# Causal decay attention and a leaky-ReLU MLP in one kernel: another order for the list of operations, with other engines for some of them

## The chip, the cores and the metric

The kernel runs on one core of a Trainium2 chip. The time is the device time of one execution in microseconds, taken as the median of the runs shown. The core has five engines that run at once, each through its own instructions in order: TensorE (PE, with weight loads PEld), VectorE (DVE), ScalarE (ACT), GpSimd (POOL) and SyncE (SP), which here only issues DMAs. ACT and POOL issue DMAs too.

## What is computed

Attention with a decay per head (4 batches, 8 heads, 768 positions, head width 64) gives 3072 rows of 512 numbers; a two-layer MLP (512 to 2048 to 512) with a leaky ReLU is applied to them.

```python
for b in range(nb):                       # blocks of 64 positions
    intra = einsum('bhic,bhjc->bhij', qb, kb) * Dmask[None]
    intra = einsum('bhij,bhjd->bhid', intra, vb)
    inter = einsum('bhid,bhde->bhie', qb * lam_pow[None], kv_state)
    out[:, :, sl] = intra + inter
    kv_state = lam_block * kv_state + einsum('bhsd,bhse->bhde', kb * rev_pow[None], vb)
x = out.transpose(0, 2, 1, 3).reshape(3072, 512)
h = x @ w_in
g = maximum(h, 0.0) + alpha * minimum(h, 0.0)
return g @ w_out
```

Dmask holds lam to the power of the distance where it is not negative, and zero elsewhere; the other factors are powers of lam as well.

## The kernel before

**Tiling.** The tokens are worked in six chunks c of 512: 256 positions of two batches. The attention of a chunk is four units: two batches times two halves of the heads. There are 24 units, numbered through, so units 8 to 11 are chunk 2. A unit has two blocks of 128 positions, 0 and 1.

**One unit** goes through these steps. `load` (fp32) and `load16` (fp16) bring k, q and v in; a `hold` is a one-element write that keeps a load from starting before a place in DVE's list. `cast` makes one fp16 tile `qk16` of q and k. `turn_by_dma` transposes it with a DMA issued by SP into `qkT` (units 0 to 7 use `turn` on PE and a copy, `turned`). `decayed` scales the transposed q into `qdT`, `key_decayed` scales k into `kdec`. `cluster(old, new)` is a run of small matmuls in a PSUM tile `acc`: for the old unit the state part (from `RD` and `qdT`) and the product of masked scores with v, for the new unit the scores `s` and the state's increment. `masked` multiplies the scores by the decay mask, `state` makes the next state `R`, `spread` copies it into `RD`, and `out_of` copies a unit's result from PSUM into `xT`, the MLP's input.

**The MLP of a chunk**: for each of 16 tiles f of the hidden layer, `up` (four matmuls into one PSUM bank), `below` (ACT: the negative part), `gate` (DVE: the leaky ReLU in fp16). A bank is free for the next `up` once its `gate` is done. For chunks 0 to 2 `down` makes the second layer, a quarter of the sum a call, and `store` copies and sends the result. For chunks 3 to 5 the second layer is seven `product`s a pair of blocks instead of eight, for which sums of blocks of g and of w_out are needed: `weight_sum`, `weight_less`, `gate_sum`, or `gate_copied` and `gate_added` (the same sum made by DMAs, the second issued by POOL). `taken` copies or adds a product's PSUM into the result and issues the stores.

**What sets the order.** Nothing is scheduled by the program. The list of operations at the end of the function (from L659) is the order: each engine gets its own instructions in the order in which the list names them, and waits, inside an instruction, for what its data need. Last arguments choose the engine: "V" is DVE, "A" is ACT, "G" is POOL; a load with `ring=1` goes by POOL, without it by SP. The list's opening, to L795, is the same before and after but for one `hold`.

```python
def copy_on(eng, out, in_):              # casts, spreads, out_of, turned
    if eng == "A": nc.scalar.activation(out, in_, AF.Copy)
    elif eng == "V": nc.vector.tensor_copy(out=out, in_=in_)
    else: nc.gpsimd.tensor_copy(out=out, in_=in_)
```

`warm_up` writes a one on DVE and takes its logarithm on ACT (L179), for which ACT loads a function table; its result is read by nothing.

Of the kernel before, what the change touches and what calls it, by code (L numbers as in the profile page):

```python
# [11 lines left out]
def kernel(  # L12
# [434 lines left out]
    G = {}  # L447
# [322 lines left out]
    masked(3, 0)  # L770
    spread(3, 1, "A", True)
# [60 lines left out]
    below(0, 1, 1)
    below(0, 7, None)
    masked(4, 0)
    load_wout(0)
    decayed(4, "G")
    gate(0, 1, 1)
    gate(0, 7, None)
    up(0, 9, None, 0)
    below(0, 9, None)  # L840
    cluster(4, 5)
    masked(5, 1)
    gate(0, 9, None)
    up(0, 11, None, 2)
    below(0, 11, None)
    gate(0, 11, None)
    state(5, 0)
    cast(6, "k", "G")
    zeros(3, 0)
    state(5, 1)  # L850
    up(0, 14, None, 1)
    load("q", 2, 0, ring=1)
    spread(5, 1, "A")
    below(0, 14, None)
    gate(0, 14, None)
    decayed(5, "G")
    up(0, 12, None, 0)
    up(0, 10, None, 2)
    masked(5, 0)
    below(0, 10, None)  # L860
    turn(6)
    up(0, 15, None, 1)
    out_of(4, "A")
    cluster(5, None)
    key_decayed(6, "G")
    gate(0, 10, None)
    cast(7, "k", "V")
    up(0, 13, None, 2)
    below(0, 12, None)
    turned(6, "V")  # L870
    below(0, 15, None)
    out_of(5, "A")
    turn(7)
    gate(0, 12, None)
    load_wout(2)
    up(1, 0, 0, 0)
    below(0, 13, None)
    cluster(None, 6)
    below(1, 0, 0)
    gate(0, 15, None)  # L880
    down(0, 2, 0, 1)
    gate(1, 0, 0)
    up(1, 2, 0, 0)
    gate(0, 13, None)
    below(1, 2, 0)
    hold("k", 2, 1)
    turned(7, "A")
    down(0, 2, 1, 2)
    masked(6, 1)
    up(1, 1, 0, 2)  # L890
    state(6, 0)
    load_wout(3)
    gate(1, 2, 0)
    decayed(6, "G")
    key_decayed(7, "V")
    below(1, 1, 0)
    gate(1, 1, 0)
    cast(9, "q", "V")
    decayed(7, "V")
    down(0, 1, 0, 0)  # L900
    spread(6, 1, "A")
    cast(9, "k", "V")
    down(0, 1, 1, 2)
    masked(6, 0)
    down(0, 0, 0, 2)
    down(0, 0, 1, 1)
    down(0, 0, 2, 1)
    state(6, 1)
    down(0, 1, 2, 2)
    cluster(6, 7)  # L910
    out_of(6, "A")
    down(0, 0, 3, 1)
    cast(8, "k", "V")
    load("k", 2, 1, ring=1)
    spread(9, 0, "V")
    load16("v", 2, 0)
    state(7, 0)
    cast(8, "q", "V")
    down(0, 2, 2, 2)
    down(0, 2, 3, 2)  # L920
    turn_by_dma(8)
    store(0, 0)
    spread(7, 1, "A")
    key_decayed(8, "G")
    store(0, 2)
    up(1, 3, 0, 2)
    below(1, 3, 0)
    masked(7, 0)
    masked(7, 1)
    state(7, 1)  # L930
    cast(10, "k", "V")
    weight_sum(1, 0)
    cluster(7, 8)
    masked(8, 1)
    key_decayed(9, "G")
    gate(1, 3, 0)
    down(0, 1, 3, 2)
    out_of(7, "A")
    up(1, 4, None, 1)
    turn_by_dma(9)  # L940
    store(0, 1)
    state(8, 0)
    below(1, 4, None)
    decayed(8, "G")
    load("q", 2, 1)
    key_decayed(10, "G")
    masked(8, 0)
    spread(8, 1, "G")
    up(1, 5, None, 0)
    state(8, 1)  # L950
    cluster(8, 9)
    below(1, 5, None)
    load("q", 3, 0)
    cast(11, "k", "V")
    up(1, 0, 1, 2)
    gate(1, 4, None)
    below(1, 0, 1)
    gate(1, 5, None)
    up(1, 1, 1, 1)
    below(1, 1, 1)  # L960
    gate(1, 0, 1)
    cast(10, "q", "A")
    up(1, 6, None, 0)
    cast(11, "q", "V")
    down(0, 3, 0, 2)
    gate(1, 1, 1)
    up(1, 7, None, 1)
    below(1, 6, None)
    load16("v", 3, 0)
    weight_sum(1, 1)  # L970
    down(0, 3, 1, 2)
    below(1, 7, None)
    gate(1, 6, None)
    masked(9, 1)
    load16("v", 2, 1)
    key_decayed(11, "V")
    up(1, 8, None, 0)
    state(9, 0)
    below(1, 8, None)
    down(0, 3, 2, 2)  # L980
    down(0, 3, 3, 2)
    turn_by_dma(10)
    cast(12, "q", "V")
    load("k", 3, 0)
    masked(9, 0)
    gate(1, 8, None)
    up(1, 11, None, 0)
    spread(9, 1, "A")
    decayed(9, "G")
    gate(1, 7, None)  # L990
    turn_by_dma(11)
    out_of(8, "V")
    store(0, 3)
    up(1, 10, None, 1)
    spread(13, 0, "A")
    decayed(10, "V")
    key_decayed(12, "G")
    below(1, 11, None)
    state(9, 1)
    below(1, 10, None)  # L1000
    cast(12, "k", "V")
    up(1, 13, None, 2)
    gate(1, 11, None)
    cluster(9, 10)
    below(1, 13, None)
    up(1, 9, None, 0)
    gate(1, 10, None)
    load("k", 4, 0)
    below(1, 9, None)
    up(1, 15, None, 1)  # L1010
    gate(1, 13, None)
    state(10, 0)
    load("k", 3, 1)
    load("q", 4, 0)
    gate(1, 9, None)
    below(1, 15, None)
    up(1, 12, None, 2)
    turn_by_dma(12)
    below(1, 12, None)
    up(1, 14, None, 0)  # L1020
    gate(1, 15, None)
    masked(10, 0)
    out_of(9, "A")
    cast(13, "q", "G")
    down(1, 0, 0, 1)
    below(1, 14, None)
    gate(1, 12, None)
    cast(13, "k", "G")
    down(1, 0, 1)
    decayed(11, "G")  # L1030
    up(1, 2, 1, 2)
    gate(1, 14, None)
    up(1, 3, 1, 0)
    down(1, 0, 2)
    spread(11, 0, "G")
    down(1, 0, 3)
    below(1, 3, 1)
    cast(14, "k", "G")
    key_decayed(13, "G")
    spread(10, 1, "V")  # L1040
    state(10, 1)
    spread(10, 0, "A")
    masked(10, 1)
    cluster(10, 11)
    spread(14, 0, "V")
    load("q", 3, 1)
    key_decayed(15, "G")
    gate(1, 3, 1)
    below(1, 2, 1)
    gate(1, 2, 1)  # L1050
    state(11, 0)
    cast(16, "k", "A")
    masked(11, 0)
    spread(11, 1, "V")
    state(11, 1)
    load("q", 5, 0)
    turn_by_dma(13)
    masked(11, 1)
    out_of(10, "A")
    store(1, 0)  # L1060
    down(1, 2, 0, 2)
    load("q", 4, 1, ring=1)
    cast(16, "q", "G")
    decayed(13, "G")
    cast(15, "k", "V")
    down(1, 2, 1)
    down(1, 2, 2)
    turn_by_dma(16)
    down(1, 2, 3)
    store(1, 2)  # L1070
    cluster(11, 12)
    warm_up()
    down(1, 1, 0, 1)
    down(1, 1, 1)
    spread(12, 0, "G")
    state(12, 0)
    spread(12, 1, "V")
    out_of(11, "A")
    up(2, 2, None, 2)
    decayed(12, "G")  # L1080
    up(2, 0, None, 0)
    down(1, 1, 2)
    down(1, 1, 3)
    state(12, 1)
    below(2, 0, None)
    cast(14, "q", "A")
    below(2, 2, None)
    key_decayed(16, "V")
    load16("v", 3, 1)
    masked(12, 1)  # L1090
    weight_sum(2, 0)
    cast(17, "q", "G")
    store(1, 1)
    gate(2, 0, None)
    up(2, 3, None, 0)
    gate(2, 2, None)
    up(2, 1, None, 1)
    below(2, 1, None)
    masked(12, 0)
    gate(2, 1, None)  # L1100
    key_decayed(14, "G")
    cluster(12, 13)
    weight_sum(2, 1)
    below(2, 3, None)
    gate(2, 3, None)
    cast(15, "q", "G")
    down(1, 3, 0, 2)
    load("k", 4, 1)
    state(13, 0)
    up(2, 4, None, 1)  # L1110
    turn_by_dma(14)
    cast(18, "q", "G")
    cast(19, "k", "A")
    below(2, 4, None)
    down(1, 3, 1)
    turn_by_dma(15)
    key_decayed(17, "V")
    down(1, 3, 2)
    masked(13, 1)
    gate(2, 4, None)  # L1120
    up(2, 5, None, 0)
    up(2, 6, None, 1)
    out_of(12, "A")
    spread(13, 1, "G")
    cast(19, "q", "V")
    below(2, 5, None)
    state(13, 1)
    below(2, 6, None)
    masked(13, 0)
    gate(2, 5, None)  # L1130
    cluster(13, 14)
    spread(15, 0, "G")
    up(2, 7, None, 0)
    gate(2, 6, None)
    below(2, 7, None)
    state(14, 0)
    load("k", 5, 1)
    state(14, 1)
    down(1, 3, 3)
    up(2, 8, None, 1)  # L1140
    out_of(13, "A")
    masked(14, 1)
    store(1, 3)
    masked(14, 0)
    below(2, 8, None)
    decayed(14, "G")
    spread(18, 0)
    gate(2, 7, None)
    spread(14, 1, "G")
    gate(2, 8, None)  # L1150
    cluster(14, 15)
    up(2, 9, None, 2)
    load("k", 5, 0)
    masked(15, 0)
    state(15, 0)
    up(2, 10, None, 0)
    below(2, 9, None)
    load16("v", 4, 0)
    up(2, 11, None, 1)
    below(2, 10, None)  # L1160
    gate(2, 9, None)
    turn_by_dma(19)
    gate(2, 10, None)
    up(2, 12, None, 2)
    decayed(15, "G")
    out_of(14, "A")
    key_decayed(19)
    state(15, 1)
    spread(15, 1, "A")
    up(2, 13, None, 0)  # L1170
    below(2, 12, None)
    masked(15, 1)
    below(2, 11, None)
    below(2, 13, None)
    gate(2, 12, None)
    load16("v", 5, 1)
    cluster(15, 16)
    gate(2, 11, None)
    out_of(15, "A")
# [396 lines left out]
```

## Time and profile before

| | |
|---|---|
| median of 3 runs | 214.49 us (213.87 to 215.24) |
| profiled execution, its own time | 213.43 us |
| its span, first to last instruction | 211.6 us |
| TensorE clock granted | 1.0 throughout |
| POOL busy after 160 us | 0.00 us |
| busy share of the 16 DMA engines, about 5 to 116 us | 0.8 to 0.9 and more in every slice |
| HBM read, written | 27.28 MB, 6.29 MB |

Busy shares of a span are averages over stages; "idle before" and the waits say what an engine stood for. A matmul's listed time includes the pipeline that the next one overlaps: four matmuls of 512 columns list 1.0 us together and follow the four before them by 0.86 to 0.88 us.

### The profile page before, as it was taken

What the parts mean: (1) busy time and instruction counts of PE and PEld (TensorE: products, weight loads), DVE (VectorE), ACT (ScalarE), POOL (GpSimd) and SP (SyncE); (2) the same over time, 40 slices, a digit from 0 to 9 for tenths busy, and PEclk for the clock granted to TensorE, in tenths of its full rate; (3) what the DMA queues carried; (4) which work ended last, traced back from release to release, by engine and by line L of the source; (5) the groups of instructions that cost most, each with busy time, mean ns of one, the idle gap of its engine ahead of it and who ended that gap; (6) DMA issues with size and microseconds to landing.
All of it is one profiled execution on the core that took longest, in us unless ns stands there. A gap on an engine that the chain in (4) does not pass through costs nothing.

```text
span 211.6 us, 5657 instructions
## 1 busy us (share of the span) xinstructions
PE 200.9 (95%) x2286; PEld 124.6 (59%) x2286; DVE 168.9 (80%) x347; ACT 112.7 (53%) x231; POOL 83.5 (39%) x122
## 2 busy tenths in 40 slices
PE   4798999999999999999999999999999999999992
PEld 4776555555555455455544545556666766766881
DVE  3799799999689994889988969999669778549731
ACT  3998576643647536455755556363464525354320
POOL 8989199170721570987960083213021000000000
PEclk9999999999999999999999999999999999999999
DMA  4999999998999999899999391867273211011213
GB/s 113 275 184 194 198 237 227 246 245 118 276 238 220 314 222 231 247 152 243 135 208 105 121 222 56 156 149 157 41 187 65 99 53 50 2 50 53 74 53 124
DMA packets 62443, 33.54 MB, mean 158 GB/s; under 512 B 34497, under 2 KB 58577, under 8 KB 62417
## 3 DMA queue, kind: packets, MB, share of 16 engines
q0 software_dynamic: 22096, 12.45, 41.1%
q1 hardware_dynamic: 38416, 17.57, 35.8%
q10 hardware_dynamic: 1904, 3.16, 4.4%
q8 instruction: 18, 0.29, 0.6%
q14 instruction: 9, 0.07, 0.1%
HBM read 27.28 MB, written 6.29 MB: 159 GB/s over the span
## 4 chain that ended last, share of the span: by engine, by line
PE 78%; ACT 9%; DVE 6%; DMA 4%; issue 2%; ACTq 0%; DVEq 0%; SPq 0%
PE h_ps L457 36%; PE p_ps L598 17%; PE o_ps L491 15%; PE s L362 3%; DVE g L481 3%; PE acc L374 2%; DMA qkT<-qk 2%; DMA lam_sb<-in_lam_dram 2%; ACT qkT L248 2%; PE acc L344 2%; ACT dmask L202 1%; DVE RD L250 1%; ACT qk L248 1%; PE acc L391 1%; DVE sm L403 1%
## 5 line engine op out<-in xcount | busy, mean ns | idle before, releaser
L457 PE MATMUL h_ps<-xT,w_in_sb 128*128 128x512 f16 (+1 forms) x416 | 92.8, 363 | 1.0 <-DVE g L481 0.6
L468 ACT ACTIVATE m<-h_ps 128x512 f32<-128x512 f32 (+1 forms) x104 | 57.5, 564 | 59.9 <-PE h_ps L457 55.0
L481 DVE SCALAR_TENSOR_TENSOR g<-m,oma,h_ps 128x512 f16<-128x512 f32 (+1 forms) x104 | 71.1, 702 | 19.3 <-ACT m L468 18.2
L457 PEld LDWEIGHTS <-w_in_sb 128*128 128x128 f16 x416 | 39.3, 98 | 38.9 <-issue 1.8
L491 PE MATMUL o_ps<-w_out_sb,g 128*128 128x512 f16 x192 | 45.9, 379 | 0.2 <-DVE g L481 0.2
L403 DVE TENSOR_TENSOR sm<-s,dmask 128x512 f16<-128x512 f32 x48 | 32.1, 684 | 2.2 <-PE s L362 2.1
L491 PEld LDWEIGHTS <-g 128*128 128x128 f16 x192 | 18.2, 98 | 20.7 <-issue 0.2
L321 POOL TENSOR_TENSOR qdT<-qkT,qdecay 128x512 f16<-128x512 f16 (+1 forms) x16 | 17.5, 1096 | 16.8 <-DMA qkT<-qk 13.0
L598 PEld LDWEIGHTS <-g 128*128 128x128 f16 x192 | 18.8, 98 | 4.8
L279 POOL TENSOR_TENSOR kdec<-kraw,kdecay 128x512 f16<-128x512 f32 x13 | 13.7, 1063 | 8.4 <-DMA kraw<-in_k_dram 8.3
L428 DVE SCALAR_TENSOR_TENSOR R<-R,rdecay,acc 128x64 f16<-128x64 f16 x60 | 13.8, 272 | 3.7 <-PE acc L391 1.9
L598 PEld LDWEIGHTS <-gsum 128*128 128x128 f16 x144 | 14.0, 98 | 3.1
L252 POOL COPY RD<-R 64x128 f16<-64x128 f16 x24 | 7.8, 324 | 16.2 <-DVE R L428 15.5
L622 ACT ACTIVATE o_sb<-p_ps 128x512 f32<-128x512 f32 (+1 forms) x16 | 7.6, 489 | 10.8 <-PE p_ps L598 10.8
L248 ACT ACTIVATE xT<-acc 128x512 f16<-128x512 f32 x15 | 8.9, 596 | 8.0 <-PE acc L391 5.4
L238 PE MATMUL op_fill<-ident 128*128 128x128 f16 x109 | 9.3, 253 | 3.0 <-POOL ident masks.py:199 2.7
L598 PE MATMUL p_ps<-wsum,gsum 128*128 128x256 f16 x96 | 12.0, 273 | 0.0
L598 PE MATMUL p_ps<-wsum,g 128*128 128x256 f16 x96 | 11.9, 272 | 0.0
L248 ACT ACTIVATE RD<-R 64x128 f16<-64x128 f16 x28 | 8.6, 306 | 6.1 <-DVE R L428 4.9
L598 PE MATMUL p_ps<-w_out_sb,g 128*128 128x256 f16 x96 | 11.6, 273 | 0.0
L102 POOL DMA_DIRECT2D vh<-in_v_dram x13 | 11.5, 890 | 0.0
L238 PEld LDWEIGHTS <-ident 128*128 128x128 f16 x109 | 8.4, 116 | 3.5 <-POOL ident masks.py:199 2.7
(87 smaller groups left out, 215.4 us busy)
## 6 DMA issues: line engine op xcount, KB each, us to landing
kraw<-in_k_dram SPq DMA_DIRECT2D x8, 512.0 KB, 5.7
out_dram<-o_sb ACTq DMA_DIRECT2D x12, 256.0 KB, 3.1
qraw<-in_q_dram SPq DMA_DIRECT2D x6, 512.0 KB, 7.3
out_dram<-o_sb SPq DMA_DIRECT2D x24, 128.0 KB, 2.0
vh<-in_v_dram POOLq DMA_DIRECT2D x11, 256.0 KB, 6.2
w_in_sb<-in_moe_w_in_dram POOLq DMA_DIRECT2D x4, 512.0 KB, 9.4
w_out_sb<-in_moe_w_out_dram POOLq DMA_DIRECT2D x4, 512.0 KB, 9.5
gsum<-g SPq DMA_DIRECT2D x6, 256.0 KB, 2.6
```

Of the source, the lines that this page charges most:

```text
L102: nc.gpsimd.dma_start(out=rows16(x, c, bi)[:, ds(h0, n), :], in_=source({"q": q, "v": v}[x], c, bi, h0, n))
L238: nc.tensor.matmul(t[:, 0:128], lhsT=ident, rhs=ident, start=True, stop=True)
L248: nc.scalar.activation(out, in_, AF.Copy)
L279: engine(eng).tensor_tensor(out=kdec, in0=kr, in1=d.unsqueeze(3).to_broadcast([128, 2, 4, D]), op=ALU.mult)
L321: engine(eng).tensor_tensor(out=x, in0=y, in1=d.unsqueeze(2).to_broadcast([128, 4, n, 64]), op=ALU.mult)
L403: nc.vector.tensor_tensor(out=t["sm"][hl], in0=t["s"][hl], in1=mask_of(hl, units[n][2]), op=ALU.mult)
L428: nc.vector.scalar_tensor_tensor(out=then[:, hp], in0=R[b, hh, i][:, hp], scalar=rdecay[:, 2 * hh + hp : 2 * hh + hp + 1], in1=kv[:, hp], ...
L457: nc.tensor.matmul(h_ps[:, 0:n] if bi is None else h_ps[:, 0:n].rearrange("p (e j) -> p e j", e=2), lhsT=w_in_sb[:, gi, ts(f, 128)], rhs=x ...
L468: nc.scalar.activation(m[:, 0:n], HP[c, f, bi][:, 0:n], AF.Relu, scale=-1.0)
L481: nc.vector.scalar_tensor_tensor(out=g, in0=mv, scalar=oma[:, f : f + 1], in1=hv, op0=ALU.mult, op1=ALU.add)
L491: nc.tensor.matmul(O[c, t], lhsT=gated(c, f)[:, t // 2, t % 2, :], rhs=w_out_sb[:, f, :], start=(f == 0), stop=(f == NF - 1),)
L598: nc.tensor.matmul(acc, lhsT=lhsT, rhs=rhs, start=(first and j == 0), stop=(j == NJ - 1), skip_group_check=True,)
```

## The change

The list past the opening is written in another order, and some operations change engine. No operation's arithmetic changes.

- Casts: 11 leave DVE (5 to ACT, 6 to POOL), 2 come to it. Copies of states (`spread`, two instructions each): 8 leave DVE, 2 come to it.
- `decayed`: 6 go from DVE to POOL. `key_decayed`: 5 go from DVE to POOL, 4 the other way. `out_of`: 4 each way between DVE and ACT.
- `weight_sum`: 4 of 8, and `gate_sum`: 5, go from DVE to POOL; 3 `gate_added` become `gate_sum` on DVE.
- `warm_up` is no longer called.
- The last result of the last chunk is that of product 4, copied by ACT, in place of two of product 3, added by DVE.
- Loads of w_out and of k and q of chunks 2 to 5 stand at other places in POOL's and SP's lists.

```diff
+    spread(9, 0, "V")
     gate(0, 3, 0)
+    cast(5, "q", "V")
...
-    cast(9, "q", "V")
-    decayed(7, "V")
...
+    cast(8, "k", "A")
+    cast(9, "k", "G")
+    decayed(7, "G")
...
-    weight_sum(1, 1)
...
-    warm_up()
...
+    weight_sum(1, 1, "G")
...
+    gate_sum(4, 3, 1, "k", eng="G")
...
+    product(5, 3, 0, None, True)
+    taken(5, 4, 1)
+    taken(5, 3, 0)
     product(5, 4, 0, None, True)
-    taken(5, 5, 1)
-    taken(5, 5, 0)
-    product(5, 3, 0, None, True)
     taken(5, 4, 0)
-    product(5, 3, 1, None, True)
-    taken(5, 4, 1)
-    taken(5, 3, 1)
-    taken(5, 3, 0)
```

The list after, at the place where chunk 0's last tiles and the units 4 to 6 meet (before, `below(0, 11)` and `gate(0, 11)` followed `up(0, 11)` at once, with the `state` and `spread` of unit 5 behind them):

```python
gate(0, 9, None); cast(6, "k", "G"); state(5, 0); up(0, 11, None, 2)
spread(5, 1, "A"); state(5, 1); up(0, 14, None, 1); up(0, 12, None, 0)
below(0, 11, None); masked(5, 0); gate(0, 11, None); below(0, 14, None); gate(0, 14, None)
up(0, 10, None, 2); masked(5, 1); out_of(4, "A"); below(0, 10, None); cast(7, "k", "V")
up(0, 15, None, 1); gate(0, 10, None); turn(6); below(0, 12, None); below(0, 15, None)
cluster(5, None); turned(6, "V"); out_of(5, "A"); up(0, 13, None, 2); gate(0, 12, None)
```

**SP's queue, from the first DMA transposes on, before.** The four transposes are those of units 8, 9, 10 and 11; qraw and kraw are loads of q and k.

```order
L305 DMA_TRANSPOSE qkT_1249<-qk16_1232 128x8x128
L305 DMA_TRANSPOSE qkT_1345<-qk16_1137 128x8x128
L89 DMA qraw_1356<-in_q_dram 128x8x128
L89 DMA qraw_1428<-in_q_dram 128x8x128
L305 DMA_TRANSPOSE qkT_1503<-qk16_1273 128x8x128
L89 DMA kraw_740<-in_k_dram 128x8x128
L305 DMA_TRANSPOSE qkT_1521<-qk16_1430 128x8x128
```

The same stretch of SP's queue after, again units 8, 9, 10 and 11.

```order
L305 DMA_TRANSPOSE qkT_1239<-qk16_1003 128x8x128
L89 DMA qraw_1263<-in_q_dram 128x8x128
L305 DMA_TRANSPOSE qkT_1383<-qk16_1092 128x8x128
L89 DMA qraw_1452<-in_q_dram 128x8x128
L89 DMA kraw_1472<-in_k_dram 128x8x128
L305 DMA_TRANSPOSE qkT_1526<-qk16_1261 128x8x128
L89 DMA kraw_1618<-in_k_dram 128x8x128
L89 DMA qraw_1621<-in_q_dram 128x8x128
L305 DMA_TRANSPOSE qkT_1641<-qk16_1247 128x8x128
```

One load now stands between the transposes of units 8 and 9, two (one of them k of chunk 4) in front of unit 10's, and two in front of unit 11's.

**ACT's queue around the table load, before.** o_sb rows are `store`s of chunk 1, xT is `out_of`, m is `below`.

```order
L511 ACTIVATE o_sb_1785<-o_ps_1653 128x512
L512 DMA out_0_dram<-o_sb_1785 128x512
L511 ACTIVATE o_sb_1785<-o_ps_1788 128x512
L512 DMA out_0_dram<-o_sb_1785 128x512
L179 ACT_TABLE_LOAD
L179 ACTIVATE warm_140<-one_139 128x1
L248 ACTIVATE xT_1523<-acc_1816 128x2x4x64
L468 ACTIVATE m_1911<-h_ps_1896 128x512
```

The same stretch of ACT's queue after (RD rows are a `spread` of unit 19).

```order
L511 ACTIVATE o_sb_1781<-o_ps_1661 128x512
L512 DMA out_0_dram<-o_sb_1781 128x512
L248 ACTIVATE xT_1516<-acc_1701 128x2x4x64
L248 ACTIVATE qk16_1766<-kraw_742 128x512
L248 ACTIVATE xT_1516<-acc_1808 128x2x4x64
L511 ACTIVATE o_sb_1781<-o_ps_1774 128x512
L512 DMA out_0_dram<-o_sb_1781 128x512
L248 ACTIVATE RD1_1_134<-R1_1_4_109 64x2x64 x2
L468 ACTIVATE m_1898<-h_ps_1889 128x512
```

The load and the logarithm are gone, the `out_of` of unit 11 stands ahead of the second store instead of behind it, and a cast of unit 13 is new here.

**POOL's queue in the stretch of chunk 3's products, after.** gsum_2747 and gsum_2774 are the two chained sums of blocks of g, wsum_2949 is one of w_out's sums, kdec and qdT are keys and queries of units 22 and 21.

```order
L578 DMA gsum_2747<-g_2373 128x1024
L279 TENSOR_TENSOR kdec_2929<-kraw_2134,kdecay_155 128x512
L252 CAST qk16_2761<-qraw_1937 128x512
L545 TENSOR_TENSOR wsum_2949<-w_out_sb_90 128x1024
L321 TENSOR_TENSOR qdT_2968<-qkT_2437,qdecay_157 128x512
L578 DMA gsum_2747<-g_2373 128x1024
L545 TENSOR_TENSOR wsum_2949<-w_out_sb_90 128x1024
L578 DMA gsum_2774<-gsum_2747 128x1024
L252 COPY RD2_1_136<-R2_1_5_120 64x2x64 x2
L578 DMA gsum_2774<-gsum_2747 128x1024
```

Before, POOL's queue held in that place only DMAs, short copies and one `key_decayed`:

```order
L279 TENSOR_TENSOR kdec_2744<-kraw_2228,kdecay_155 128x512
L252 COPY RD1_1_134<-R1_1_5_110 64x2x64 x2
L578 DMA gsum_2566<-gsum_2519 128x1024
L578 DMA gsum_2519<-g_2376 128x1024
L578 DMA gsum_2566<-gsum_2519 128x1024
L578 DMA g_2376<-g_2376 128x1024
```

Two sums of 128x1024, a cast and two scalings now stand between the DMAs that make the sums of g.

More of the change, by code (lines that the diff above doesn't have):

```diff
@@ L879 @@
     below(1, 0, 0)
-    gate(0, 15, None)
     down(0, 2, 0, 1)
+    load16("v", 2, 0)
+    up(1, 1, 0, 2)
     gate(1, 0, 0)
[L883 to L895, printed above, removed]
     below(1, 1, 0)
     gate(1, 1, 0)
-    cast(9, "q", "V")
-    decayed(7, "V")
+    turn(7)
+    cast(9, "q", "A")
@@ L938 @@
[L938 to L962, printed above, removed]
@@ L986 @@
[L986 to L1003, printed above, removed]
+    cluster(7, 8)
+    store(0, 2)
+    down(0, 1, 3, 2)
+    gate(1, 3, 0)
+    out_of(7, "A")
+    store(0, 1)
@@ L1036 @@
[L1036 to L1056, printed above, removed]
-    turn_by_dma(13)
-    masked(11, 1)
-    out_of(10, "A")
@@ L1060 @@
[L1060 to L1071, printed above, removed]
-    warm_up()
[L1073 to L1081, printed above, removed]
+    key_decayed(13, "G")
+    load("k", 3, 1)
@@ L1151 @@
     cluster(14, 15)
     up(2, 9, None, 2)
-    load("k", 5, 0)
-    masked(15, 0)
[L1155 to L1173, printed above, removed]
+    gate(2, 7, None)
```

982 lines of the change are left out of this document (545 added, 437 removed).

## The prediction

> **What bounds the kernel now.** I read the page's busy times first, then a table of windows for where TensorE stands still, then the chain and the engines' timelines at those places. All shares are averages over stages, so the page's line only says where to look.
>
> ```profile
> PE 200.9 (95%) x2286; PEld 124.6 (59%) x2286; DVE 168.9 (80%) x347; ACT 112.7 (53%) x231; POOL 83.5 (39%) x122
> ```
>
> TensorE is busy 200.9 of 211.6 us, so it is idle for 10.7. The windows below (length, then busy us of PE, PEld, DVE, ACT, POOL, then clock, DMA share, GB/s) hold all of that.
>
> ```profile
> 0.00:23.00 23.00, 17.34 (x350) 14.71 (x351) 17.94 (x48) 18.46 (x45) 18.89 (x34) 1.00 1.23 192
> 28.00:33.00 5.00, 4.66 (x36) 2.58 (x34) 4.95 (x12) 3.43 (x7) 4.90 (x7) 1.00 1.34 255
> 53.00:54.00 1.00, 0.64 (x18) 0.44 (x19) 0.00 (x0) 0.57 (x1) 0.07 (x1) 1.00 1.05 279
> 77.00:79.00 2.00, 1.78 (x56) 1.21 (x54) 1.97 (x7) 0.34 (x1) 1.56 (x3) 1.00 1.16 295
> 87.00:89.00 2.00, 1.79 (x9) 0.68 (x8) 2.00 (x4) 1.44 (x3) 2.00 (x2) 1.00 0.47 141
> 207.70:211.60 3.90, 0.01 (x1) 0.00 (x0) 0.76 (x2) 0.00 (x0) 0.00 (x0) 1.00 0.30 101
> ```
>
> The opening, which the change leaves as it is, has 5.66; the end, behind the last matmul, 3.89; and the 185 us between have 0.34 + 0.36 + 0.22 + 0.21 = 1.13 in four places. The number of matmuls is the same after, at a clock of 1.00 before. So the most that another order can win is these 1.13, a part of the 3.89, and short waits that the overlap of matmuls hides from the busy time, for which I allow 0.4: about 2.1 us together (1.13 + 0.6 + 0.4, the 0.6 from the end, below), 1% of the time. What it can lose has no such limit.
>
> **The change part by part.**
>
> *Unit 8's transpose (53 to 54).* The chain gives issue to landing; the matmul row shows PE waiting for it.
>
> ```profile
> 50.01 3.79 DMA qkT<-qk
> ```
>
> ```profile
> 53.84 0.42 PE L362 MATMUL s<-qkT 64*64 64x128 f16 x16 [0.36 <-DMA qkT<-qk]
> ```
>
> Before, the casts of unit 8 stood behind others in DVE's list, and SP could issue at 50.01, 3.5 us ahead of the need. After, q is cast by POOL early and k by ACT, behind `out_of(6)` and `state(7, 0)`.
>
> ```profile
> L248 ACT ACTIVATE xT<-acc 128x512 f16<-128x512 f32 x15 | 8.9, 596 | 8.0 <-PE acc L391 5.4 <-DVE R L428 2.5
> ...
> L248 ACT ACTIVATE qk<-kraw 128x512 f16<-128x512 f32 x5 | 3.1, 623 | 0.0
> ...
> L425 ACT ACTIVATE R<-acc 128x128 f16<-128x128 f32 x6 | 1.7, 277 | 0.0
> ```
>
> ```profile
> 63.64 1.73 PE o_ps L491 x8
> ```
>
> From the end of `cluster(6, 7)` ACT needs 0.60 + 0.28 + 0.62 = 1.5 us. PE has seven quarters of `down` (1.73 / 2 = 0.865 each), a half `up` (0.43, half of that) and the state part (some 0.2) before it needs the transposed tile: 6.7 us. That leaves 5.2 for a transfer that took 3.79: the 0.36 goes.
>
> *The table load (87 to 89).* On ACT:
>
> ```profile
> 82.71 1.28 ACT L179 ACT_TABLE_LOAD   x1 [0.40 <-ACT o_sb L511]
> 84.01 0.20 ACT L179 ACTIVATE warm<-one 128x1 f32<-128x1 f32 x1
> 84.12 0.58 ACT L248 ACTIVATE xT<-acc 128x512 f16<-128x512 f32 x1
> ```
>
> ```profile
> 87.43 0.67 DVE g L481
> 88.10 0.04 issue
> 88.14 1.02 PE h_ps L457 x4
> ```
>
> The load holds `out_of(11)` back by 84.12 - 82.71 = 1.4 us, `state(12, 1)` on DVE waits for that (its row, L428 below, names ACT's xT), and behind it on DVE stands the gate that frees PE's bank at 88.10. More than the 0.21 of idle is taken off that chain, so the 0.21 goes and the rest meets PE, which is then the bound. The Trainium skill ("ScalarE: Activation LUTs", What ACT_TABLE_LOAD costs) has 1.28 us for the load and 1.38 more for a drain behind it, 2.66 together; here the next operation starts 0.02 us behind the load, so the trace has 1.28 alone. By either figure the sum is the same, since PE's idle time limits it.
>
> *Less on DVE (77 to 79).* The net moves, by these rows:
>
> ```profile
> L481 DVE SCALAR_TENSOR_TENSOR g<-m,oma,h_ps 128x512 f16<-128x512 f32 x88 | 63.9, 743 | 16.3 <-ACT m L468 15.4
> L403 DVE TENSOR_TENSOR sm<-s,dmask 128x512 f16<-128x512 f32 x48 | 32.1, 684 | 2.2 <-PE s L362 2.1
> L428 DVE SCALAR_TENSOR_TENSOR R<-R,rdecay,acc 128x64 f16<-128x64 f16 x60 | 13.8, 272 | 3.7 <-PE acc L391 1.9 <-ACT xT L248 1.7
> ...
> L570 DVE TENSOR_TENSOR gsum<-g,gsum 128x1024 f16<-128x1024 f16 x8 | 5.4, 687 | 0.1
> L250 DVE CAST qk<-kraw 128x512 f16<-128x512 f32 x13 | 5.4, 419 | 0.4 <-DMA kraw<-in_k_dram 0.3
> ...
> L321 DVE TENSOR_TENSOR qdT<-qkT,qdecay 128x512 f16<-128x512 f16 x6 | 4.1, 685 | 0.0
> ```
>
> Nine casts at 0.419, six `decayed` at 0.685 and, net of the three that come, six sums at 0.687 make 3.8 + 4.1 + 4.1 = 12.0 us off DVE's 168.9. Almost none of it is on the path now, since PE stood for DVE only in the rows above. It takes the 0.22 at 77 to 79, where DVE was busy 1.97 of 2.00. POOL gets them.
>
> ```profile
> L321 POOL TENSOR_TENSOR qdT<-qkT,qdecay 128x512 f16<-128x512 f16 x10 | 12.9, 1293 | 13.4 <-DMA qkT<-qk 13.0
> ```
>
> A sum of 1024 columns on POOL has no row before: at least this 1.29 for 512, at most twice it, 2.59. I take 2.4, near the upper end, because the work is per element. Six `decayed` (7.8) and nine sums (11.6 to 23.3) bring POOL from 83.5 to 103 to 115, half the span. In the stretch of chunk 3's products the sums of g end with a DMA that POOL issues:
>
> ```profile
> gsum<-gsum POOLq DMA_DIRECT2D x4, 256.0 KB, 3.9
> ```
>
> From `weight_sum(4, 1)` up to that DMA POOL's queue holds two more such sums (3 x 2.4 = 7.2), three `decayed` (3.9), a scaling, a cast and two DMA issues (about 1 each), 15, and 3.9 more to the landing: 19. PE has 20 `up`s, `down`s and products (0.865) and three clusters (about 1.2 each), 21 us, before `product(3, 6)` needs it: 2 us to spare.
>
> *28 to 33.* The wait there is for a gate, and after, `spread(9, 0)` and `cast(5, "q")` stand in front of the gates instead of behind them. Followed gate by gate, PE loses about 0.4 at `up(0, 0, 1)` in place of 0.34 at `up(0, 7)`. I count no change (between -0.3 and +0.3).
>
> *The end.* The last product's result now passes ACT once instead of DVE twice, and one store is issued behind it instead of two.
>
> ```profile
> 207.74 0.76 DVE L620 TENSOR_TENSOR o_sb<-p_ps,o_sb 128x256 f32<-128x256 f32 x2 [2.13 <-PE p_ps L598]
> ```
>
> ```profile
> L622 ACT ACTIVATE o_sb<-p_ps 128x256 f32<-128x256 f32 x8 | 2.9, 382 | 7.7 <-PE p_ps L598 7.7
> ```
>
> 0.76 becomes 0.38; the second issue saves a little more where it queued. I take 0.5 (0.4 to 0.6).
>
> *New tight places.* Three banks serve the `up`s, so a bank has two others' `up`s, 1.73 us, for its `below` and `gate` (0.60 + 0.74 = 1.34): 0.39 to spare. After, at tiles 11 to 13 of chunk 0, `spread(5, 1)` on ACT and `masked(5, 0)`, then `turned(6)`, on DVE stand in front of gates; `masked` has 0.68 by its row, and the others are taken as like it, so each is some 0.3 too long, where clusters and turns do not give PE other work. I count 0.4 (0 to 1.0). And unit 10: from the end of `cluster(8, 9)` DVE does two `state`s, a half gate, two `masked`, a gate and the cast (4 x 0.27 + 0.48 + 2 x 0.68 + 0.74 + 0.42 = 4.1, the half gate taken as 0.74 less 0.27), and only then can SP issue. PE's work up to the need is the same as before but for one half `up`:
>
> ```profile
> 58.16 1.91 PE L457 MATMUL h_ps<-xT,w_in_sb 128*128 128x256 f16 x12
> ...
> 68.23 0.42 PE L362 MATMUL s<-qkT 64*64 64x128 f16 x16
> ```
>
> 68.23 - 58.16 - 0.43 = 9.6, less an allowance of 0.2 for waits hidden in it: 9.4. So 5.3 us are left for a transfer that in this stretch (50 to 70 us) took
>
> ```profile
> DMA to landing us min/median/max: 3.8/5.3/8.1
> ```
>
> and by the order two more loads stand in front of it. I count 0.3 (0 to 2.8).
>
> The sum: -0.36 - 0.21 - 0.22 - 0.5 + 0.4 + 0.3 = -0.6. The profiled execution took 213.43 with its launch and end, 1.06 less than the median of 214.49; -0.6 on 213.43 is 212.8, and on the median 213.9.
>
> **The rivals.** 1% of 214.49 is 2.1 us; the runs before spread by 1.4, so less than 1% cannot well be told from no change. The bounds are 212.35 and 216.6.
>
> *All of it comes and nothing is given back.* 1.13 + 0.6 + 0.4 of hidden waits is 2.1: 212.4, just at the bound. For it: DVE gets 12 us lighter. Against: DVE's lighter load can only show in 0.22 + 0.34 us. Chance of more than 1%: 0.11.
>
> *It is all given back* in bank waits and at unit 10, at the upper ends of what I counted: 214.5 to 215.5. Chance 0.13.
>
> *Late transposes, the slower case.* The DMA engines are full until about 116 us, and SP's queue now puts loads ahead of the transposes of units 9, 10 and 11. A landing of 8.1 at unit 10, as the slowest of this stretch, is 2.8 late: 213.9 - 0.3 + 2.8 = 216.4, and with unit 8 or 11 late too it is above 216.6. It is slower than before from a landing of 6.2 on. For it: the wait at 53.84 shows that this resource does end waits. Against: most landings are nearer 5, and unit 8's is helped. Chance 0.12, of which 0.08 above 1%.
>
> *POOL holds DVE up.* The trace has it once clearly.
>
> ```profile
> 45.16 2.02 DVE L250 CAST qk<-qraw 128x512 f16<-128x512 f32 x1
> ```
>
> ```profile
> 44.83 2.06 POOL L279 TENSOR_TENSOR kdec<-kraw,kdecay 128x512 f16<-128x512 f32 x2
> ```
>
> A cast of 0.42 took 2.02 and ended with two POOL scalings, 1.6 us of delay. After, POOL is busier by 20 to 31 us with longer operations. Where such a cast stands in front of a gate, the bank's 0.39 covers a part and 1.2 us remain. One makes the kernel slower than 213.9 would be, to 215.1; three make 217.5, over the bound. The place would be the casts of units 10 and 11 and the sums of chunk 3. The Trainium skill ("Advanced Engine Details and Errata", VectorE Performance Modes) says that VectorE's second SBUF port is shared with GpSimd, so that GpSimd's instructions and two-port VectorE ones block each other; by that rule the change's move to POOL costs more than its rows, and the trace agrees in this row. Against: DVE keeps few copies from SBUF (half its casts leave), and its gates, which read PSUM, keep 743 on the mean beside all of POOL's work. Chance 0.09, all above 1%.
>
> **How the numbers follow.** Forecast 213.9, between 212.4 and 214.5: chance 0.55. Faster than 1%: 0.11. Within 1%: 0.55 + 0.13 + 0.04 = 0.72. Slower: 0.08 + 0.09 = 0.17. For 8 in 10 the range begins at the limit of what can be won, 212.4, and reaches to the one late transpose, 216.3; about 0.1 is left out on each side.
>
> **What would show it.** In the windows after, the idle places at 53 and 87 are gone and no ACT_TABLE_LOAD stands behind the opening; PE's idle between 23 us and the last matmul is 1 us or less, at other places; behind the last matmul one ACT copy of 0.38 and one store. DVE's busy time falls to about 153 to 157, POOL's rises to 103 to 115, its sums of 1024 columns at 2.4. A wait of PE for `qkT` at unit 10 or 11 shows the third rival, DVE copies of over 1 us beside POOL's sums in front of PE's waits for gates the fourth. The forecast is wrong if PE's idle after 23 us differs from 1.1 by more than 2 us, or if the matmuls themselves change cadence.

## The result and the profile after

The changed kernel takes 223.01 us, the median of four runs, where the kernel before takes 214.18 us: a ratio of 1.040, with a 95% interval from 1.034 to 1.047. The prediction was 213.9, with a range up to 216.3. The profiled execution took 223.33 us, its span is 221.0 us (before 211.6), 9.4 more. Of the executions in the next section three (218.19 us of ten, 225.04 of nine, 223.01 of six) ran at a lower clock and over 1.5% above the fastest of their kernel; they are in the medians and in no ratio.

The page of the changed kernel, busy times first: as before, they only say where to look.

```profile
PE 202.6 (92%) x2286; PEld 125.9 (57%) x2286; DVE 166.5 (75%) x311; ACT 116.6 (53%) x244; POOL 109.9 (50%) x142
```

PE has 1.7 us more of busy time for the same matmuls, and DVE, which has 36 instructions fewer, is down by only 2.4 us. The list of what PE waited for (total, times, longest) gives the place at once:

```profile
PE s L362 <- DVE sm L403: 7.3, 1, 7.3
PE op_fill L238 <- POOL ident masks.py:199: 2.7, 1, 2.7
PE acc L391 <- DMA vh<-in_v_dram: 1.3, 1, 1.3
PE tp L291 <- ACT qkT L248: 1.1, 1, 1.1
PE acc L374 <- issue: 0.5, 1, 0.5
```

The second and fourth are the opening's, as before (2.7 and 1.0). The first is one wait of 7.3 us, the third one of 1.3, and the fifth a pause in the opening, at 17.1 us (before, 0.3 at 22.7); what the list has besides is 0.5 or less each. The chain of waits around the first, in order of time:

```profile
136.63 0.66 DVE g L481
137.29 8.59 DVE kdec L279
145.87 0.61 DVE sm L403
146.49 0.04 issue
146.53 0.64 PE s L362 x12
```

PE waits for the masked scores of unit 19, `masked(19, 0)`, which stand behind `key_decayed(23, "V")` in DVE's queue. That one scaling took 8.67 us. Beside it, DVE's row and what POOL did meanwhile (start, duration):

```profile
137.20 8.67 DVE L279 TENSOR_TENSOR kdec<-kraw,kdecay 128x512 f16<-128x512 f32 x1
```

```profile
136.94 1.67 POOL L279 TENSOR_TENSOR kdec<-kraw,kdecay 128x512 f16<-128x512 f32 x1
137.94 1.22 POOL L252 CAST qk<-qraw 128x512 f16<-128x512 f32 x1
138.51 2.71 POOL L545 TENSOR_TENSOR wsum<-w_out_sb 128x1024 f16<-128x1024 f16 x1
140.58 1.75 POOL L321 TENSOR_TENSOR qdT<-qkT,qdecay 128x512 f16<-128x512 f16 x1
141.68 1.48 POOL L578 DMA_DIRECT2D gsum<-g  x1
142.29 3.02 POOL L545 TENSOR_TENSOR wsum<-w_out_sb 128x1024 f16<-128x1024 f16 x1
```

This is the run of POOL that the order showed ahead of the prediction: scaling, cast, sum, scaling, DMA issue, sum. The last sum ends at 142.29 + 3.02 = 145.31, and DVE's scaling 0.56 later, at 145.87. So the scaling ended when POOL's run did. That it was this run that held it, and not its keys or its buffer, is for the experiments to show.

What follows the wait costs more. Windows of the same trace (length, then busy us of PE, PEld, DVE, ACT, POOL, then clock, DMA share, GB/s):

```profile
0.00:23.00 23.00, 16.82 (x325) 13.85 (x326) 17.17 (x45) 17.57 (x43) 19.26 (x34) 0.93 1.24 192
...
140.00:144.00 4.00, 0.00 (x0) 0.00 (x0) 4.00 (x1) 0.00 (x0) 4.00 (x4) 0.82 1.07 225
144.00:148.00 4.00, 1.47 (x41) 1.27 (x41) 3.27 (x4) 0.16 (x1) 2.14 (x2) 0.50 0.67 117
148.00:152.00 4.00, 4.00 (x21) 2.02 (x20) 1.37 (x6) 1.71 (x4) 0.00 (x0) 0.83 0.19 68
```

```profile
134.73 0.42 PE L362 MATMUL s<-qkT 64*64 64x128 f16 x16
...
135.42 3.63 PE L491 MATMUL o_ps<-w_out_sb,g 128*128 128x512 f16 x16
...
147.74 1.82 PE L491 MATMUL o_ps<-w_out_sb,g 128*128 128x512 f16 x4
149.40 1.89 PE L457 MATMUL h_ps<-xT,w_in_sb 128*128 128x512 f16 x8
```

The granted clock falls to 0.50 while PE stands, and is back at full behind the four matmuls of `down`. From the scores to the next `down` the cluster takes 135.42 - 134.73 = 0.69 us at full clock and 147.74 - 146.53 = 1.21 behind the wait; the four matmuls of `down` take 149.40 - 147.74 = 1.66 in place of 0.865. That is 0.52 + 0.80 = 1.3 us. In the opening, whose list is the same, the clock was 0.93 in this execution, where before had 1.00, and the scores of unit 4, the first place past it, start at 27.84 us in place of 26.48. More than half of that is there already at unit 2's scores (17.72 in place of 16.98), behind the pause of 0.5 us, for which the profile shows no cause; the rest comes behind it, with the clock. The six other traces with nearly the changed list have 26.62 to 26.96 us for unit 4. By the mean clocks three of the four executions had such a clock in the opening: they have 0.977, and the fourth, the shortest at 221.83 us, has 0.984. Why it came in three is not shown.

The account of the span: 7.3 (wait) + 1.3 (half clock behind it) + 1.3 (v) + about 1.3 (the opening's pause and clock) = 11.2, less the 1.6 us of span that the change wins (worked out at the end of the section on why the prediction was wrong): 9.6, and 9.4 was measured.

### The profile page after: what moved, and what is told of

The parts are those of the page before. It is cut to its first block, busy times and chain, and to the rows that moved or that the text cites. A ratio compares the mean times of both kernels' runs of the same rounds, so it can differ in the third digit from the quotient of the medians.

```text
span 221.0 us, 5669 instructions
## 1 busy us (share of the span) xinstructions
PE 202.6 (92%) x2286; PEld 125.9 (57%) x2286; DVE 166.5 (75%) x311; ACT 116.6 (53%) x244; POOL 109.9 (50%) x142
## 4 chain that ended last, share of the span: by engine, by line
PE 75%; DVE 9%; DMA 7%; POOL 2%; issue 2%; ACT 2%; POOLq 0%; DVEq 0%; ACTq 0%
PE h_ps L457 33%; PE p_ps L598 17%; PE o_ps L491 15%; DVE kdec L279 5%; DMA vh<-in_v_dram 4%; PE s L362 3%; DMA qh<-in_q_dram 2%; PE acc L374 2%; DVE g L481 2%; PE acc L344 2%; PE acc L391 1%; DVE sm L403 1%; POOL wsum L545 1%; PE tp L291 1%; DVE dmask L207 1%
## 5 line engine op out<-in xcount | busy, mean ns | idle before, releaser
L321 POOL TENSOR_TENSOR qdT<-qkT,qdecay 128x512 f16<-128x512 f16 (+1 forms) x22 | 24.1, 1097 | 24.2 <-DMA qkT<-qk 16.6
L362 PE MATMUL s<-qkT 64*64 64x128 f16 x384 | 10.5, 229 | 7.3 <-DVE sm L403 7.3
L252 POOL COPY RD<-R 64x128 f16<-64x128 f16 x24 | 6.9, 289 | 19.2 <-DVE R L428 18.5
L279 DVE TENSOR_TENSOR kdec<-kraw,kdecay 128x512 f16<-128x512 f32 x10 | 15.6, 1557 | 0.1
L279 POOL TENSOR_TENSOR kdec<-kraw,kdecay 128x512 f16<-128x512 f32 x14 | 15.2, 1090 | 0.3
L570 POOL TENSOR_TENSOR g<-g 128x1024 f16<-128x1024 f16 x2 | 4.2, 2125 | 17.8 <-DVE gsum L570 17.8
L248 ACT ACTIVATE RD<-R 64x128 f16<-64x128 f16 x40 | 12.2, 305 | 1.1 <-ACT o_sb L511 0.4
L362 PEld LDWEIGHTS <-qkT 64*64 64x64 f16 x384 | 6.6, 110 | 10.0 <-issue 7.8
```

Of the source, the lines that this page charges most:

```text
L279: engine(eng).tensor_tensor(out=kdec, in0=kr, in1=d.unsqueeze(3).to_broadcast([128, 2, 4, D]), op=ALU.mult)
L321: engine(eng).tensor_tensor(out=x, in0=y, in1=d.unsqueeze(2).to_broadcast([128, 4, n, 64]), op=ALU.mult)
L362: nc.tensor.matmul(s[hl][ds(a * 64, 64), hp, 1 - e, :].rearrange("p (e j) -> p e j", e=2), lhsT=t["qkT"][p, 1, e, hp, ds(a * 64, 64)], rhs ...
```

## The experiments

**Theory A.** A DVE instruction whose operands all lie in SBUF is held for as long as POOL runs one instruction after another. **Theory B**: the order as a whole is slower, by several waits. **Theory C**: the scaling waits for its own keys or its buffer. **Theory D**: only one POOL instruction can hold it, which is close to what the prediction's fourth rival had priced, 1.6 us.

**The scaling on POOL.**

```diff
-    key_decayed(23, "V")
+    key_decayed(23, "G")
```

> The changed kernel with key_decayed(23) given to POOL instead of DVE, at the same place in the list. Theory A (DVE's instruction with two SBUF inputs is held for as long as POOL runs one instruction after another): the 8.67 us instruction is gone from DVE, PE's 7.3 us wait for the masked scores behind it and the half clock that follows (4 matmuls of 0.865 us took 1.66 to 1.8) go too; the time falls from 223.0 by 8 to 10 us to 213 to 215. Theory B (the order as a whole is slower, by several waits of the same size): the time stays above 219. Theory C (the scaling waits for its own k or its buffer): POOL stands for 8 us in DVE's place, its sums of g come late and the time stays above 219.

**The scaling on DVE, earlier in the list.**

```diff
+    key_decayed(23, "V")
     weight_sum(2, 1)
...
-    key_decayed(23, "V")
```

> The changed kernel with key_decayed(23) still on DVE but some 35 operations earlier in the list, ahead of weight_sum(2, 1), where POOL's queue waits (about 122 to 131 us). Theory A: it takes 0.68 us there, no instruction of DVE is over 2.2 us, and the time is 213 to 215, as with the scaling on POOL. Theory B: above 219. Theory C: it takes over 5 us at the earlier place as well and PE stands there; 219 to 223.

Measured: 217.55 us, ratio 1.018 (1.012 to 1.024), and 217.03 us, 1.012 (1.006 to 1.019). Some 6 us of 8.8 are won, but both miss A's 213 to 215, and the 219 and more of B and C too. The trace of the second says why. Its DVE and its list of waits:

```profile
139.51 4.74 DVE L250 COPY RD<-R 64x128 f16<-64x128 f16 x2
```

```profile
PE acc L344 <- DVE RD L250: 2.5, 1, 2.5
```

With the scaling away, the next instructions of DVE with operands in SBUF alone are the two copies of `spread(20, 1, "V")`. In the changed kernel, where they ran behind POOL's run, they took 0.39 us together. POOL's run is the same; its last sum ends at 144.00, and the copies end at 144.25. PE now waits for them. In the first of the two kernels the same copies took 5.22 us and PE waited 3.0. So C falls (the scaling took 0.68 us at its earlier place), and the hold has passed on. It holds a copy with one input as well.

**The hold passed on no further.** The same with that copy given to ACT; POOL keeps its whole run.

```diff
-    spread(20, 1, "V")
+    spread(20, 1, "A")
```

> The changed kernel with key_decayed(23) ahead of weight_sum(2, 1), as before in the run with the scaling moved earlier, and with spread(20, 1), the copy that was then held for 4.5 us, given to ACT. POOL keeps both sums and its whole run. Theory A (only what DVE has with operands in SBUF alone is held, and the hold passes on to the next such instruction): between 137 and 144 us DVE has then only gates, masked scores and states, which read PSUM; the 2.5 us wait for RD and the half clock behind it go and the time is 212.8 to 214. Rival (POOL's longer run itself makes the kernel late, by its sums or scaled queries): the time stays at 216 to 217.5, with a wait at another place.

Measured: 213.19 us, ratio 0.996 (0.993 to 0.9995). DVE in the stretch of the run:

```profile
137.00 1.29 DVE L403 TENSOR_TENSOR sm<-s,dmask 128x512 f16<-128x512 f32 x2 [1.77 <-PE s L362]
138.20 0.46 DVE L428 SCALAR_TENSOR_TENSOR R<-R,rdecay,acc 128x64 f16<-128x64 f16 x2
140.66 0.75 DVE L481 SCALAR_TENSOR_TENSOR g<-m,oma,h_ps 128x512 f16<-128x512 f32 x1 [2.00 <-ACT m L468]
141.80 0.75 DVE L481 SCALAR_TENSOR_TENSOR g<-m,oma,h_ps 128x512 f16<-128x512 f32 x1 [0.39 <-ACT m L468]
142.46 0.68 DVE L250 CAST xT<-acc 128x512 f16<-128x512 f32 x1
```

Masked scores, states, gates and the copy out of PSUM keep their durations beside a POOL that is busy throughout; each has one operand in PSUM. Two operations of DVE in another place, with no change on POOL, turn 223 us into 213.2. The order as a whole is not slower than before, so B falls.

**A shorter run on POOL.**

```diff
-    weight_sum(3, 0, "G")
+    weight_sum(3, 0)
...
-    weight_sum(3, 1, "G")
+    weight_sum(3, 1)
```

> The changed kernel with weight_sum(3, 0) and weight_sum(3, 1) given back to DVE, key_decayed(23) left on DVE. POOL's run behind the scaling's start is then shorter by the two sums: it ends near 140.5 instead of 145.3. Theory A: the scaling ends with the run, so it takes 3 to 4 us, PE waits 2 to 3 us instead of 7.3, and the time is 216 to 218. Theory D (only one POOL instruction holds it): what was seen was something else and the scaling stays near 8 us, or falls to under 1.5 at once. Theory C: it stays at 8.7 us and the time at 223.

Measured: 213.53 us, ratio 0.997 (0.994 to 1.0003), better than A's 216 to 218. The scaling took 1.96 us, which is neither A's 3 to 4 nor D's 8 or under 1.5. The row of the scaling, and POOL beside it:

```profile
135.10 1.96 DVE L279 TENSOR_TENSOR kdec<-kraw,kdecay 128x512 f16<-128x512 f32 x1
```

```profile
134.83 1.67 POOL L279 TENSOR_TENSOR kdec<-kraw,kdecay 128x512 f16<-128x512 f32 x1
135.82 1.69 POOL L252 CAST qk<-qraw 128x512 f16<-128x512 f32 x1
```

POOL's scaling ends at 136.50 and DVE's 0.56 later, at 137.06, with POOL's cast behind it, which took 1.69 in place of 1.22: here DVE got its turn between two POOL instructions. In the changed kernel it arrived just as late behind the start of the same POOL instruction (137.20 to 136.94, here 135.10 to 134.83) and did not get it. So it is not always the whole run that holds DVE. The sums that were taken away stood behind the place at which the scaling was let in; why that let it in is not shown.

**A run of POOL in the kernel before.**

```diff
-    spread(20, 1, "A")
+    spread(20, 1, "G")
+    decayed(20, "G")
...
-    weight_sum(4, 0)
+    weight_sum(4, 0, "G")
...
-    weight_sum(3, 0)
-    decayed(20, "V")
+    weight_sum(3, 0, "G")
```

> The kernel before, with spread(20, 1), decayed(20), weight_sum(4, 0) and weight_sum(3, 0) given to POOL, so that POOL runs from about 137 to 143 us without a pause beside DVE's key_decayed(23) and key_decayed(21), at 138.5. Theory A: the scaling of unit 23 takes 4 to 5 us instead of 0.68, the gate behind it comes late, and the time grows by 1 to 4 us. Theory B (the hold belongs to the changed order): both scalings keep 0.68 and the time stays within 0.7 us of before.

Measured: 216.89 us, ratio 1.015 (1.009 to 1.020), 2.5 us more. The time is as A says, the hold is not: the scaling of unit 23 took 0.73 us, not 4 to 5, and it was the two operations behind it that were held. Again the rows show turns, one for each POOL instruction:

```profile
139.76 3.25 DVE L279 TENSOR_TENSOR kdec<-kraw,kdecay 128x512 f16<-128x512 f32 x2
142.93 2.61 DVE L321 TENSOR_TENSOR qdT<-qkT,qdecay 128x512 f16<-128x512 f16 x1
```

```profile
139.90 2.57 POOL L545 TENSOR_TENSOR wsum<-wsum,w_out_sb 128x1024 f16<-128x1024 f16 x1
142.43 2.56 POOL L545 TENSOR_TENSOR wsum<-w_out_sb 128x1024 f16<-128x1024 f16 x1
```

The two scalings of k took 0.73 and 2.60 us (3.25 from the first's start to the second's end, in place of 1.4), the scaling of q 2.61 in place of 0.68, and each POOL sum 2.57 in place of 2.11. PE waited 3.0 us for gates. This is the slowest of the four executions (218.32 us). So a run of POOL holds DVE in the kernel before as well, here by one instruction at a time.

**The hold by itself, by form.** A kernel that does nothing else: an instruction of DVE beside five scalings of POOL (in four trials three sums).

> A measurement by itself; it computes nothing of the reference and fills the result with zeros. In each trial ACT writes a small tile for which both DVE and POOL wait; POOL then runs five scalings like key_decayed (about 1.05 us each) one after another, with no, one or two DMA issues (adding to a tile, as gate_added does) ahead of them; DVE runs a short copy and one to three casts out of PSUM, and then the instruction under test, so that it starts in the first or second scaling. Forms under test: the scaling (kdec), a cast, a copy of 64x128 (RD), a sum of 1024 columns (wsum), all with operands in SBUF alone; and with one operand in PSUM the cast of out_of (xT), masked (sm) and the gate. Theory A1 (operands in SBUF alone are held, and DVE gets its turn at the end of each POOL instruction unless POOL has taken its next one already, as it has behind two DMA issues): xT, sm and gate keep 0.68 to 0.75 everywhere; the other four take 1 to 1.7 us with no issue ahead and 3 to 5 us, the whole run, with two. Theory A2 (held to the end of the run always): 3 to 5 us in all three. Theory A3 (one POOL instruction at most): under 1.8 us in all three. If the number of SBUF inputs decides, kdec and wsum are held, cast and copy are not.

Rows of DVE, grouped (count, busy us, mean ns): alone, and in a run with no DMA issue ahead.

```profile
L75 DVE TENSOR_TENSOR kdec_clean<-kraw,kdecay 128x512 f16<-128x512 f32 x3 | 16.0, 5329 | 0.0
...
L93 DVE COPY copy_clean<-R 64x128 f16<-64x128 f16 x3 | 14.4, 4802 | 0.0
...
L91 DVE CAST cast_clean<-kraw 128x512 f16<-128x512 f32 x2 | 9.4, 4716 | 0.0
...
L99 DVE SCALAR_TENSOR_TENSOR gate_clean<-m,oma,acc 128x512 f16<-128x512 f16 x2 | 1.5, 732 | 0.0
...
L97 DVE TENSOR_TENSOR sm_clean<-acc,dmask 128x512 f16<-128x512 f32 x2 | 1.4, 676 | 0.0
...
L75 DVE TENSOR_TENSOR kdec_alone<-kraw,kdecay 128x512 f16<-128x512 f32 x1 | 0.7, 674 | 0.0
...
L93 DVE COPY copy_alone<-R 64x128 f16<-64x128 f16 x1 | 0.2, 174 | 0.0
```

A copy of 0.174 us takes 4.8. All 28 trials with operands in SBUF alone ended behind the last POOL instruction of the run, by some 0.05 us for the copy, 0.29 for the cast and 0.55 for the others, alike with none, one or two DMA issues ahead. The 18 with an operand in PSUM kept 0.67 to 0.74. A1 and A3 fall here, A2 holds, and so it is not the number of SBUF inputs that decides: the cast and the copy have one.

**The hold by itself, by the run.** Does the kind of POOL instruction, the moment of arrival or traffic open a gap?

> A second measurement by itself; it computes nothing of the reference and fills the result with zeros. The instruction under test is DVE's scaling of 0.67 us (in 'three' two scalings and a sum), started at five different moments 0.1 us apart, beside a POOL run of a scaling, a cast, a sum of 1024 columns and a scaling ('mixed'; with two DMA issues ahead, 'issues'; with four loads of 1 MB under way, 'traffic'), three such sums ('sums' and 'three') or six casts ('casts'). Theory A2 (held to the end of the run, as all 30 held trials of the first measurement were): the scaling ends 0.55 us behind POOL's last instruction in every trial, so 4 to 6 us in 'mixed', 5 to 6 in 'sums', 3 in 'casts', and in 'three' the first alone is held. Theory A1 (DVE gets a turn at a boundary between POOL instructions, as it did beside the two sums in the kernel before with a POOL run): under 2.7 us in most trials of the kinds where it holds, and in 'three' each of the three waits for one sum. If loads under way open a gap, 'traffic' is shorter than 'mixed'.

```profile
L77 DVE TENSOR_TENSOR three_a<-kraw,kdecay 128x512 f16<-128x512 f32 x5 | 29.9, 5984 | 0.0
L77 DVE TENSOR_TENSOR sums_a<-kraw,kdecay 128x512 f16<-128x512 f32 x5 | 29.9, 5981 | 0.0
...
L77 DVE TENSOR_TENSOR casts_a<-kraw,kdecay 128x512 f16<-128x512 f32 x5 | 15.6, 3118 | 0.0
...
L77 DVE TENSOR_TENSOR three_b<-kraw,kdecay 128x512 f16<-128x512 f32 x5 | 3.4, 679 | 0.0
```

A2 again: 29 of 30 were held to the end of the run, and in "three" the first alone was held. In the thirtieth, the first of "mixed", a copy ahead of the scaling was held in its place (1.24 us), so the scaling began behind the run and took 0.68. The loads meant for "traffic" ran, on SP's own queue, in the stretch of "mixed" and "sums", so it is those two that were beside traffic; they show no gap either. With the 28 above (not 30, as the expectation has it), 57 of 57 that met the run were held to its end.

**The table load alone.** The kernel before without `warm_up`.

```diff
-    warm_up()
```

> The kernel before without warm_up, the table load in the middle of the list, alone. By the prediction's term the 0.21 us of idle at 87 to 89 us go and nothing else: ratio about 0.999. Rival: the 1.28 us of ACT are on the path in full, ratio 0.994. Second rival: another load is made at another place, ratio 1.000.

Measured: 213.87 us, ratio 0.999 (0.997 to 1.001). The full 1.28 us on the path (0.994) is excluded; the 0.21 us of the prediction agrees, but cannot be told from nothing.

**What is left of the change when the hold is gone.** Sums on DVE and the scaling earlier, both at once; then the loads of v for units 14 and 15 and for 16 and 17 exchanged as well (the list of changes leaves out that the loads of v moved too: the changed list has that of 16 and 17 ahead of that of 14 and 15).

> The changed kernel with weight_sum(3, 0) and (3, 1) on DVE and key_decayed(23) moved ahead of weight_sum(2, 1): both mends in one. Theory A: no instruction of DVE is over 2.2 us behind 130 us and PE's 0.6 us wait for the masked scores goes: 212.5 to 213.5, at or a little under the run with the sums alone (213.5), 0.4 to 0.9% under before. Theory B (other waits of the changed order are as large): 213.5 or more.

```diff
-    load16("v", 4, 0)
+    load16("v", 3, 1)
...
-    load16("v", 3, 1)
+    load16("v", 4, 0)
```

> The changed kernel with both mends (the sums on DVE, key_decayed(23) earlier) and the loads of v for units 14 and 15 and for units 16 and 17 in the other order on POOL, so that the first is issued near 80 us instead of 88. The last wait of over 0.3 us behind the opening (1.2 us for v at 96 us) should go: 212.0 to 212.6, ratio 0.989 to 0.992 to before. Rival: units 16 and 17 then wait for their v instead, and the time stays at 213.1 (0.995).

Measured: 213.08 us, ratio 0.995 (0.993 to 0.997), and 212.44 us, 0.992 (0.989 to 0.995). Both are faster than the kernel before, by less than 1%; the second has the lowest median of all, though its interval overlaps the first's, and its list of waits has nothing of over 0.2 us behind the opening.

## Why the prediction was wrong

The likeliest case did not come, and its total was near: where the hold is gone, by two operations of DVE, the kernel takes 213.19 us, 0.996 of before, and the forecast was 213.9 on 214.49, 0.997. Part of that is luck. Two costs that were counted, 0.7 us together, did not come, a gain of 0.34 that was counted at nothing did, and the 0.5 of the end shows in the span but hardly in the time (below).

**The step that failed** is the fourth rival's price. The prediction had the mechanism (POOL holds up DVE's work in SBUF) and half of the place ("the casts of units 10 and 11 and the sums of chunk 3": it was beside POOL's sums of chunk 3, but held a scaling in front of masked scores, not a cast in front of a gate), and gave it 1.6 us an event and a chance of 0.09. The runs showed one event of 8 us in its place (8.67 for a scaling of 0.68), and 7.3 of them as a wait of PE. The 1.6 came from the cast of 2.02 us beside two POOL scalings. The row was read as the size of the effect; but the cast had crossed the border of the two scalings and ended 0.3 us behind the second, the end of that run (47.18 to 46.89). Read as a rule, the run that the order shows in chunk 3 gives the price: a scaling 1.05, a cast 0.6, two sums at 2.1, a scaling 1.16 and a DMA issue are 8 us, on DVE's queue in front of masked scores for which PE waits. The point from which it decides is not three events: by an estimate it is one hold of some 3.4 us in front of one instruction that PE needs, the 2.7 from 213.9 to the bound of 216.6 and 0.7 to spare, since a hold of 8.0 made PE wait 7.3.

Nor does the trace of before have it "once clearly". It has it twice more, both times on the chain to an idle place of PE. The first:

```profile
75.51 1.60 DVE L250 COPY RD<-R 64x128 f16<-64x128 f16 x2
```

```profile
75.01 2.05 POOL L279 TENSOR_TENSOR kdec<-kraw,kdecay 128x512 f16<-128x512 f32 x2
```

The two copies (0.39 us alone) end 0.05 us behind POOL's scalings, and behind them on DVE stands the gate for which PE waits the 0.22 us at 77 to 79. There DVE was not full, as the prediction read it: it was held. The second is at 85.12, where a scaling took 1.11 us beside POOL's scaling of q, on the chain to the idle place at 88. So copies and scalings, too, could be seen to be held before the change, there by one POOL instruction each.

The step also took two facts as evidence against the hold that do not speak against it. "DVE keeps few copies from SBUF" is true, and one suffices. That its gates "keep 743 on the mean beside all of POOL's work" is true and holds after (PSUM operands are not held), but a gate behind a held instruction waits with it.

The Trainium skill ("SBUF — State Buffer", SBUF: two separate sides) says that whichever starts first has the shared ports for its whole instruction while the other blocks, and (Summary: rules for kernel authors) that the second is blocked until the first finishes. By that rule the scaling would have been held for at most one POOL instruction, some 2 us. In the shorter run and in the kernel before with a POOL run it was so (1.96; 2.60 and 2.61); in the changed kernel and in 57 of 57 trials it was the rest of the run, up to 6.3 us there and 8.67 here. The measurement decides. What makes DVE get its turn between two POOL instructions in some places stays open: the kind of POOL instruction, the moment of arrival, DMA issues ahead and traffic were varied, and in none of these trials did DVE get it.

**The half clock** behind the wait was in no term, as a wait of this length was in none.

**v for unit 14** was missed. Its load goes out at 88.37, as before (88.40), but takes longer to land, as the chain of the changed kernel says:

```profile
88.37 9.71 DMA vh<-in_v_dram
```

In before the same load took 5.7. With the exchange it goes out at 80.56, 7.8 us earlier, and the wait is gone. The wait is 1.3 and 1.2 us in two traces of the changed order, 0.3 and 0.2 in two more and none in the other two, so this load is near its edge. Why it takes longer to land was not tried.

**Steps that held.** The waits for unit 8's transpose, behind the table load and at 77 us are gone: none is in the list of waits. At the end there is one copy,

```profile
217.64 0.38 ACT L622 ACTIVATE o_sb<-p_ps 128x256 f32<-128x256 f32 x1 [2.24 <-PE p_ps L598]
```

and the span ends 3.4 us behind the last matmul (217.61), before 3.9: the 0.5 that was counted. But most of it is won in the span alone: the device time exceeds the span by 1.8 us before (213.43 to 211.6) and by 2.3 in the changed kernel (223.33 to 221.0) and with the copy on ACT (212.34 to 210.0), so it comes back behind the last instruction. POOL's 109.9 us lie within 103 to 115, its sums took 2.11 to 2.13 where nothing disturbed them (2.4 was taken), and no product waited for its sums, as the 2 us to spare promised. DVE's busy time without the long hold is 158.5, not 153 to 157: shorter holds of 0.4 to 1.5 us are in it, such as a sum of 0.68 that took 2.16 beside POOL's at 86.3. The sign that was named for a wrong forecast came as well: PE's idle time between 23 us and the last matmul is 8.8 us, not 1.1.

**Costs that did not come**: the 0.4 for tight banks at tiles 11 to 13 (two gaps under 0.1) and the 0.3 at unit 10. And 28 to 33 us, counted at nothing, won its 0.34. So the order, without the hold, wins 0.36 + 0.34 + 0.22 + 0.21 + 0.5 = 1.6 us of span: that of the run with the copy on ACT is 210.0, against 211.6. In time it wins 1.0 by the medians (213.19 to 214.20), about the four idle places without the end.

## What to carry to other kernels

Before giving work to POOL, look in DVE's queue for instructions whose operands all lie in SBUF, copies and casts included, and lay POOL's back-to-back run beside them: price the hold at up to the rest of the run, not at one instruction, and ask who waits behind the held one. Work with a PSUM operand goes on undisturbed, so a long POOL run belongs beside gates and masks. When a row shows an operation at five times its usual time, find the instruction with which it ended before taking its length as the price, and go through the trace for quieter cases of the same.

## What the runs showed of the hardware

The clock also fell behind shorter waits: in the kernel before with a POOL run, PE waited 1.94 us for a gate and the windows behind it have 0.58 and 0.56, while behind the 1.3 us for v the clock stayed at 1.00.

```profile
146.25 3.53 PE L457 MATMUL h_ps<-xT,w_in_sb 128*128 128x512 f16 x8 [1.94 <-DVE g L481]
```

```profile
146.00:148.00 2.00, 1.75 (x5) 0.67 (x5) 2.00 (x6) 0.62 (x2) 0.70 (x1) 0.58 0.99 228
148.00:150.00 2.00, 2.00 (x9) 0.81 (x8) 1.04 (x2) 0.79 (x2) 0.00 (x0) 0.56 0.86 148
```

The Trainium skill ("TensorE: Matmul & The Clock Gate", Part 1) has the clock fall after an idle window of about 3.4 us; a single wait of 1.94 us with full work ahead of it was enough here. It does not come every time: two other executions of this kernel (216.98 and 216.80 us) have a mean clock of 1.000, though what PE waited in them is not on record.
